# GeGLU feed-forward on one core: two pairs of f tiles share one run of plain products in the gate and up stage

## The chip, the cores and the metric

One Trainium2 chip, one core of it. The metric is the device time of one launch in microseconds. Inside a core, TensorE (PE in the profile) multiplies, with its weight loads shown as PEld; VectorE (DVE), ScalarE (ACT) and GpSimd (POOL) work elementwise; SyncE (SP) and ACT issue the transfers. The eight banks of PSUM, 128 x 512 fp32 each, hold what PE accumulates.

## The reference

```python
def _gelu(x):
    return jax.nn.gelu(x, approximate=True)
B, S, D, F = 1, 2048, 1024, 3584          # bfloat16 throughout
def reference(x, w_gate, w_up, w_down):
    return (_gelu(x @ w_gate) * (x @ w_up)) @ w_down
```

## The kernel before

**The halves.** The 2048 tokens are done in two halves (`h` = 0, 1) of 1024. Each half has a gate and up stage, which leaves `hT` = gelu(gate) x up with f on the partitions, and then a down stage (`down_group`, L703, two groups of 512 tokens) that multiplies by `w_down`. A half is two blocks of 512 tokens, kept transposed in `xT`.

**Seven products in place of eight.** Both stages cut their matrices in 2 x 2 blocks and form the result from seven block products. In the gate and up stage one such 2 x 2 problem is a *pair* of f tiles (2 x 128 columns of the weights) by the two token blocks, with D cut in two halves of four 128-row pieces. It is done once for gate (j = 0) and once for up (j = 1). The products are:

- M1 and M2, **plain**: bf16 weight blocks by bf16 `xT`;
- M5, M6, M7, M3 and M4, **of sums**: a sum of weight blocks (`s1`, `s2`, `s3`, `s4`, or a plain copy `a22`) by a sum of x blocks (`t1`, `t2`, `t3`, `b22`, `t4`), both kept as fp32r (fp32 in the profile's rows).

One product for one j is four matmuls of 128 x 128 by 128 x 512 (`mm`, L413) that accumulate in one bank. So a pair takes 2 x 2 plain products (16 matmuls) and 2 x 5 products of sums (40 matmuls). There are 14 pairs in each half; the first pair of half 0 is done apart, without sums, in `first_pair_units`.

**What happens to the products of a pair.** ACT copies M1 from its bank to bank set Q (L468); M2 accumulates on M1 where it stands, and gelu on ACT (L283) and the multiplication on DVE (L288, `mult`) take that result out. M6 accumulates on the copy in Q, and ACT copies the sum to set R (L464). M5 goes to set V and ACT copies it to a tile in SBUF (L458, `m5`). DVE adds `m5` to Q (L436), M3 accumulates there; M7 accumulates on R, DVE adds `m5` to that into V (L436); M4 accumulates on R. Each of the three results leaves through a gelu and a `mult`.

**Bank sets.** P, V, Q and R are two banks each (one for each j). Even pairs start their M1 in banks 0 and 1, odd pairs in 2 and 3, so that M2 of one pair can be held back.

**Order of PE.** The order on every engine is the order of the program (`on` chains the instructions of an engine). `pair_quads` does M1 of a pair, then M2 of the pair *before* (`pending`), and then the ten products of sums. So a run of 16 plain matmuls and a run of 40 matmuls of sums take turns once for each pair: 12 times after pair 1 of half 0, and 14 times in half 1. Most pairs take M6 ahead of M5.

**Preparing the next pair.** While PE does the products of sums of one pair, `prep` makes the sums of the next: POOL does `s1`, `s2`, `s3`, `s4` for both j, eight instructions (L385), and ACT the two copies `a22` (L398). There is one place in `s_mem` for each sum, so each can be made only when PE has read the old one.

**What rides along in half 0.** DVE also forms differences of `w_down` blocks for later (`stage_step`, L630, 42 of them, three for each of 14 units) that SP stores to `t_dram` (L632). Their inputs come by `stage_load` (L616) into three tiles of `wd_sb`. SP loads the x of the next half (`stage_x`, `store_x`). The next 512 columns of both weights come in two 1 MB transfers that ACT issues (`load_w`, L160), two pairs (one *chunk*) ahead.

**The end of a half.** In pair 13 SP loads the rows of `w_down` for the down stage (`load_b22` L554, `load_wd_rows` L550). Rows 8 to 13 and the first blocks of `b22` go over the memory of the last weight chunk, and blocks 4 to 13 of `b22` over that of the gelu results.

Of the kernel before, what the change touches and what calls it, by code (L numbers as in the profile page):

```python
# [34 lines left out]
def kernel(  # L35
# [8 lines left out]
    nc = tc.nc  # L44
# [355 lines left out]
    S_NAMES = ("s1", "s2", "s3", "s4", "a22")  # L400


    pending = []

    def pair_quads(hT, h, pair, nxt, then):

        key = (h, "p", pair)
        f0 = 2 * pair

        def mm(bank, j, lhs, rhs, start):  # L410
            for c in range(KH):
                pe(
                    nc.tensor.matmul(  # L413
                        banks[bank][:],
                        lhsT=lhs[:, c, :],
                        rhs=rhs[:, c, :],
                        start=start and c == 0,
                        stop=c == KH - 1,
                        skip_group_check=True,
                    )  # L420
                )

        def done(name):
            for f in then.get(name, ()):
                f()

        def prep(j, name):
            if nxt is not None:
                s_sum(nxt[0], nxt[1], j, name)

        def s(j, name):
            return ssum[(h, pair, j, name)]

        def add_m5(dst, src):
            dve(
                nc.vector.tensor_tensor(  # L436
                    out=banks[dst][:], in0=banks[src][:], in1=m5[j][:], op=ALU.add
                )
            )

        b11 = xT[0][:, half(0), :]
        b21 = xT[0][:, half(1), :]
        m5 = [None, None]
        g = {}
        P_, V_ = (PB, VB) if pair % 2 == 0 else (VB, PB)

        def m2():
            for j in range(2):
                mm(P_[j], j, block(key, j, 0, 1), b21, False)
                if j == 0:  # L450
                    g[0] = gelu(banks[P_[0]], nxt is None)
                else:
                    mult(hT, g[0], banks[P_[1]], f0, 0)

        def do_m5(j):
            mm(V_[j], j, s(j, "s1"), tsum["t1"], True)
            m5[j] = m_pool.tile([P, TB], F32, name=f"m5_{j}")
            act(nc.scalar.copy(out=m5[j][:], in_=banks[V_[j]][:]))  # L458
            if not eager:
                prep(j, "s1")  # L460

        def do_m6(j):
            mm(QB[j], j, s(j, "s2"), tsum["t2"], False)
            act(nc.scalar.copy(out=banks[RB[j]][:], in_=banks[QB[j]][:]))  # L464

        for j in range(2):
            mm(P_[j], j, block(key, j, 0, 0), b11, True)
            act(nc.scalar.copy(out=banks[QB[j]][:], in_=banks[P_[j]][:]))  # L468
        behind = len(pending) > 0
        eager = not behind and "m2" in then  # L470
        if behind:

            pending.pop()()
        done("m2 of last")
        if behind:
            if nxt is None:
                m2()
                done("m2")
            else:
                pending.append(m2)  # L480
            order = (do_m6, 0), (do_m6, 1), (do_m5, 0), (do_m5, 1)
        elif eager:
            m2()
            done("m2")
            order = (do_m5, 0), (do_m5, 1), (do_m6, 0), (do_m6, 1)
        else:
            pending.append(m2)
            order = (do_m5, 0), (do_m6, 0), (do_m6, 1), (do_m5, 1)
        for f, j in order:
            f(j)  # L490
            if (f, j) == (do_m6, 1):
                done("m6")
        for j in range(2):
            add_m5(QB[j], QB[j])
            if not eager:
                prep(j, "s2")
        done("m5")
        if eager:
            pool_behind_dve()
            for name in ("s1", "s2"):  # L500
                for j in range(2):
                    prep(j, name)
        for j in range(2):
            mm(RB[j], j, s(j, "s3"), tsum["t3"], False)
            add_m5(V_[j], RB[j])
            prep(j, "s3")
            if j == 0:
                g[1] = gelu(banks[V_[0]], nxt is None)
            else:
                mult(hT, g[1], banks[V_[1]], f0 + 1, 1)  # L510
        done("m7")
        for j in range(2):
            mm(QB[j], j, s(j, "s4"), tsum["b22"], False)
            prep(j, "s4")
            if j == 0:
                g[2] = gelu(banks[QB[0]], nxt is None)
            else:
                mult(hT, g[2], banks[QB[1]], f0, 1)
        done("m3")
        for j in range(2):  # L520
            mm(RB[j], j, s(j, "a22"), tsum["t4"], False)
            prep(j, "a22")
            if j == 0:
                g[3] = gelu(banks[RB[0]], nxt is None)
            else:
                mult(hT, g[3], banks[RB[1]], f0 + 1, 0)

        done("m4")

    SEQ = ("t1", "t2", "t3", "b22", "t4")
# [345 lines left out]

    for h in range(NH):
        hT = hT_pool.tile([P, KF, SH], BF16, name="hT")
        first_pair = 0
        if h == 0:
            first_pair_units(hT)
            first_pair = 1
            xs = [(tb, kd) for tb in (1, 0) for kd in range(KD)]
            new_x(1)
            stage_load(0)  # L890
            stage_load(1)
        for pair in range(first_pair, NPAIR):
            then = {}
            if pair % PPG == 0 and (pair // PPG + 1) * PPG < NPAIR:
                key = (h, pair // PPG + 1)

                if key not in chunks:
                    new_chunk(key)
                    for j, at in enumerate(("m2 of last", "m3")):
                        then[at] = [lambda j=j: load_w(key, j, 0, KD, act)]  # L900
            if h == 0 and pair < PPG:
                then = {
                    "m2": [lambda j=j: s_sum(0, pair, j, "a22") for j in range(2)]
                    + [lambda: t_sum("t4", 0, KH // 2)],
                    "m5": [lambda: t_sum("t4", KH // 2, KH)],
                }
            if h == 0 and pair >= PPG:

                n = [min(4 * (pair - PPG + d), NSTEP) for d in range(3)]
                steps = [lambda k=k: stage_step(k) for k in range(n[0], n[1])]  # L910
                new = range((n[1] + 2) // 3, (n[2] + 2) // 3)

                then["m2 of last"] = (
                    then.get("m2 of last", [])
                    + steps[:2]
                    + [lambda q=q: stage_x(hT, *q) for q in xs[:2]]
                )
                then["m7"] = [store_x] + [lambda i=i: stage_load(i) for i in new]
                then["m4"] = steps[2:]
                xs = xs[2:]  # L920
            if pair == NPAIR - 2:

                then.setdefault("m2 of last", []).extend(
                    [lambda: load_wd_rows(0, 4), lambda: load_wd_rows(4, 8)]
                )
            if 6 < pair < 11:
                i = 2 * pair - 8
                then.setdefault("m6", []).append(
                    lambda i=i: s_down(hT, 0, "s3", i, i + 2)
                )  # L930
            if pair == NPAIR - 1:
                then |= {
                    "m2 of last": [
                        lambda: load_b22(4, NS),
                        lambda: early.append(
                            wd_pool.tile([P, WDT, D], BF16, name="wd_sb")
                        ),
                        lambda: s_down(hT, 0, "s3", 0, 4),
                    ],
                    "m6": [  # L940
                        lambda: s_down(hT, 0, "s1", 4, 8),
                        lambda: t_down(0, "t1", 4, 6),
                    ],
                    "m2": [
                        lambda: load_wd_rows(8, 10),
                        lambda: load_wd_rows(10, 12),
                        lambda: load_wd_rows(12, NS),
                        lambda: load_b22(0, 4),
                    ],
                    "m7": [lambda: s_down(hT, 0, "s1", 0, 4)],  # L950
                    "m3": [lambda: t_down(0, "t1", 0, 2)],
                    "m4": [
                        lambda: t_down(0, "t2", 0, NT2),
                        lambda: t_down(0, "t1", 2, 4),
                        lambda: t_down(0, "t1", 6, 8),
                        lambda: s_down(hT, 0, "s1", 8, NS),
                        lambda: t_down(0, "t1", 8, NS),
                    ],
                }
            pair_quads(  # L960
                hT, h, pair, (h, pair + 1) if pair + 1 < NPAIR else None, then
            )

        then0 = {"m5": [lambda: s_down(hT, 0, "s3", 4, 6)]}
        then1 = {}
# [75 lines left out]
```

## Time and profile before

| | us |
|---|---|
| median of 3 runs (lowest, highest) | 539.48 (539.43, 539.6) |
| span of the profiled execution | 538.0 |
| what the runs' median has beyond that span | 1.48 |
| PE busy / PEld busy | 532.4 / 377.9 |
| DVE / ACT / POOL busy | 364.2 / 263.5 / 244.4 |
| gate and up of half 0, from pair 3 on | 43.4 to 183.2 |
| down of half 0 | 183.2 to 271.2 |
| gate and up of half 1 | 271.2 to 447.0 |
| down of half 1 | 447.0 to 538 |

The page gives a span for the profiled execution and no time of its own beyond it, so the span is set beside the runs. PE's clock is granted in full in all slices. PE's rows are the starts and modelled ends of matmuls; they overlap (a matmul of 0.39 us follows the one before by 0.23 us), so the busy share says little, and the distance between starts says how fast PE goes. A few matmul records are missing: of each run of 16 plain matmuls the trace has 15.

### The profile page before, as it was taken

The numbers are of one execution on the slowest core, as the hardware profiler recorded it, in microseconds if no ns is written. First come the engines' busy times: TensorE is split into PE (matmuls) and PEld (weight loads), VectorE is DVE, ScalarE is ACT, GpSimd is POOL, SyncE is SP. The second block draws the span as 40 slices with busy tenths as digits, with TensorE's granted clock in tenths as the row PEclk, the third lists the DMA queues.
The fourth block names the chain that finished last, engine by engine and source line by source line (L and its number), as shares of the span: only waits on it lengthen the run. The fifth ranks groups of instructions, "written<-read, shape, count | busy, mean of one in ns | idle before, by whom it ended". The sixth has DMA issues, their size and how long they took to land.

```text
span 538.0 us, 7084 instructions
## 1 busy us (share of the span) xinstructions
PE 532.4 (99%) x2352; PEld 377.9 (70%) x2388; DVE 364.2 (68%) x476; ACT 263.5 (49%) x447; POOL 244.4 (45%) x212
## 2 busy tenths in 40 slices
PE   9999999999999999999999999999999999999997
PEld 4577776666776686777776677777777766866866
DVE  1988777788775997989574334444444469969861
ACT  2555555555555329117465555555555552462280
POOL 0699877777776000000056776666777730000000
PEclk9999999999999999999999999999999999999999
DMA  9946876785815977789950405041322448677846
GB/s 205 323 128 195 207 252 185 238 262 197 291 61 200 361 239 246 237 279 308 324 171 1 156 1 158 15 142 57 100 78 80 155 133 284 220 246 252 293 141 212
DMA packets 92547, 102.70 MB, mean 191 GB/s; under 512 B 18656, under 2 KB 67424, under 8 KB 92512
## 3 DMA queue, kind: packets, MB, share of 16 engines
q1 hardware_dynamic: 69568, 80.23, 46.0%
q10 hardware_dynamic: 22944, 22.02, 13.4%
q8 instruction: 19, 0.31, 0.2%
q14 instruction: 16, 0.13, 0.1%
HBM read 85.98 MB, written 12.58 MB: 183 GB/s over the span
## 4 chain that ended last, share of the span: by engine, by line
PE 99%; issue 0%; ACT 0%; ACTq 0%
PE bank L413 63%; PE bank L703 33%; PE bank L264 3%; PE bank L202 1%; PE bank L308 0%; ACT bank L468 0%; ACT o_sb L759 0%; ACTq L468 0%
## 5 line engine op out<-in xcount | busy, mean ns | idle before, releaser
L413 PE MATMUL bank<-t_mem,s_mem 128*128 128x512 f32 x1056 | 249.6, 394 | 0.0
L413 PEld LDWEIGHTS bank<-t_mem,s_mem 128*128 128x128 f32 x1056 | 198.1, 188 | 44.1 <-DVE bank L436 0.4
L385 POOL TENSOR_TENSOR s_mem<-w_mem 128x512 fp32r<-128x512 bf16 x102 | 120.3, 1201 | 190.7 <-DVE t_mem L259 102.8
L703 PE MATMUL bank<-t_mem,s_mem 128*128 128x512 f32 (+1 forms) x548 | 127.2, 391 | 0.0
L288 DVE TENSOR_TENSOR hT<-w_mem,bank 128x512 bf16<-128x512 f32 x104 | 71.3, 687 | 79.9 <-PE bank L413 45.7
L703 PEld LDWEIGHTS bank<-t_mem,s_mem 128*128 128x128 f32 x548 | 102.4, 188 | 22.1 <-issue 0.2
L436 DVE TENSOR_TENSOR bank<-bank,m 128x512 f32<-128x512 f32 x108 | 69.9, 694 | 45.2 <-ACT m L458 43.7
L413 PE MATMUL bank<-xT,w_mem 128*128 128x512 bf16 x405 | 96.5, 380 | 1.4
L283 ACT ACTIVATE w_mem<-bank 128x512 f32<-128x512 f32 x104 | 61.8, 596 | 52.9 <-DVE bank L436 35.8
L413 PEld LDWEIGHTS <-w_mem 128*128 128x128 bf16 x432 | 40.2, 98 | 51.6 <-issue 6.8
L385 POOL TENSOR_TENSOR s_mem<-w_mem,s_mem 128x512 fp32r<-128x512 bf16 x52 | 65.8, 1285 | 0.0
L605 DVE TENSOR_TENSOR t_mem<-w_mem 128x1024 fp32r<-128x1024 bf16 x56 | 65.6, 1219 | 0.0
L385 POOL TENSOR_TENSOR s_mem<-s_mem,w_mem 128x512 fp32r<-128x512 f32 x52 | 60.9, 1192 | 0.0
L464 ACT COPY bank<-bank 128x512 f32<-128x512 f32 x54 | 30.8, 570 | 38.9 <-PE bank L413 38.9
L398 ACT CAST s_mem<-w_mem 128x512 fp32r<-128x512 bf16 x54 | 33.1, 615 | 30.6 <-PE bank L413 29.1
L675 DVE TENSOR_TENSOR s_mem<-hT 128x512 fp32r<-128x512 bf16 x52 | 34.2, 686 | 10.2 <-PE bank L703 9.4
L458 ACT COPY m<-bank 128x512 f32<-128x512 f32 x54 | 31.8, 589 | 17.5 <-PE bank L413 17.5
L703 PEld LDWEIGHTS <-hT 128*128 128x128 bf16 x224 | 21.3, 98 | 26.6 <-issue 2.1
L468 ACT COPY bank<-bank 128x512 f32<-128x512 f32 x54 | 30.7, 570 | 12.7 <-PE bank L413 12.7
L630 DVE TENSOR_TENSOR o_sb<-wd_sb,o_sb 128x512 fp32r<-128x512 bf16 x28 | 31.5, 1126 | 0.5
L768 ACT CAST o_sb<-bank 128x512 bf16<-128x512 f32 x27 | 14.8, 585 | 33.9 <-PE bank L703 33.9
L602 ACT CAST t_mem<-w_mem 128x1024 fp32r<-128x1024 bf16 x28 | 26.9, 1048 | 0.0
(45 smaller groups left out, 238.6 us busy)
## 6 DMA issues: line engine op xcount, KB each, us to landing
t_mem<-t_dram SPq DMA_DIRECT2D x56, 512.0 KB, 5.2
w_mem<-in_w_gate_dram ACTq DMA_DIRECT2D x10, 1024.0 KB, 5.5
w_mem<-in_w_up_dram ACTq DMA_DIRECT2D x10, 1024.0 KB, 5.5
wd_sb<-in_w_down_dram SPq DMA_DIRECT2D x28, 256.0 KB, 4.5
t_dram<-o_sb SPq DMA_DIRECT2D x28, 256.0 KB, 2.4
wd_sb<-in_w_down_dram SPq DMA_DIRECT2D x12, 512.0 KB, 7.7
w_mem<-in_w_down_dram SPq DMA_DIRECT2D x4, 1024.0 KB, 6.6
w_mem<-in_w_down_dram SPq DMA_DIRECT2D x8, 512.0 KB, 8.3
```

Of the source, the lines that this page charges most:

```text
L283: act(nc.scalar.activation(out=g_sb, in_=ps[:], func=ACT.Gelu_apprx_tanh))
L288: nc.vector.tensor_tensor(out=hT[:, fc, tb * TB : (tb + 1) * TB], in0=g_sb, in1=ps[:], op=ALU.mult,)
L385: pool(nc.gpsimd.tensor_tensor(out=t, in0=in0, in1=in1, op=op))
L398: act(nc.scalar.copy(out=t, in_=a(1, 1)))
L413: nc.tensor.matmul(banks[bank][:], lhsT=lhs[:, c, :], rhs=rhs[:, c, :], start=start and c == 0, stop=c == KH - 1, skip_group_check=True,)
L436: nc.vector.tensor_tensor(out=banks[dst][:], in0=banks[src][:], in1=m5[j][:], op=ALU.add)
L458: act(nc.scalar.copy(out=m5[j][:], in_=banks[V_[j]][:]))
L464: act(nc.scalar.copy(out=banks[RB[j]][:], in_=banks[QB[j]][:]))
L605: dve(nc.vector.tensor_tensor(out=t, in0=in0, in1=in1, op=ALU.subtract))
L630: dve(nc.vector.tensor_tensor(out=t, in0=in0, in1=in1, op=ALU.subtract))
L675: dve(nc.vector.tensor_tensor(out=t, in0=in0, in1=in1, op=op))
L703: nc.tensor.matmul(banks[bank][:, c0:c1], lhsT=lhs(i, u), rhs=rhs(i)[:, c0:c1], start=start and i == 0, stop=stop and i == NS - 1, skip_gr ...
```

## The change

`pair_quads` becomes `quads`, which takes both pairs of a chunk (`members`). It does M1 of both pairs and then M2 of both in one run of 32 plain matmuls, and after it the ten products of sums of the first pair and the ten of the second. `pending` is gone. Half 0 has pair 1 alone, as before, and then six such groups; half 1 has seven. The bank sets follow: in a group the first pair starts in P and copies its M1 to Q, the second starts in R and copies to V; then both use P for M5 and R for the copy of M6. All pairs take M6 ahead of M5, but for pair 1 of half 0 and the first group of half 1, which take M5 first.

What rides along is moved with it. Of the eight `stage_step` of a group four now stand on DVE behind M1 of both pairs and ahead of the two `mult` of the plain run, and two at the start of the sums of each pair (before, two stood behind M2 and two behind M4 in each pair). `stage_load` runs as tiles come free, and three are issued at the start, not two. The chunk loads, the loads of `x` and the `w_down` loads of the last two pairs stand at the start of a pair's sums ("start"), where they stood behind M2 of the pair before ("m2 of last").

```diff
-    def pair_quads(hT, h, pair, nxt, then):
+    def quads(hT, h, members, nxt, thens, m5_first):
...
+        for n, pair in enumerate(members):
+            after = (h, members[n + 1]) if n + 1 < len(members) else nxt
+            first_ = (PB, RB)[n] if len(members) > 1 else VB
+            run.append((pair, after, thens[n], first_, (QB, VB)[n]))
...
-        P_, V_ = (PB, VB) if pair % 2 == 0 else (VB, PB)
-
-        def m2():
+        for pair, _, _, first_, q_ in run:
             for j in range(2):
-                mm(P_[j], j, block(key, j, 0, 1), b21, False)
+                mm(first_[j], block((h, "p", pair), j, 0, 0), b11, True)
+                act(nc.scalar.copy(out=banks[q_[j]][:], in_=banks[first_[j]][:]))
+        done(0, "m1")
+        for pair, _, _, first_, _ in run:
+            for j in range(2):
+                mm(first_[j], block((h, "p", pair), j, 0, 1), b21, False)
                 if j == 0:
-                    g[0] = gelu(banks[P_[0]], nxt is None)
+                    g = gelu(banks[first_[0]])
                 else:
-                    mult(hT, g[0], banks[P_[1]], f0, 0)
+                    mult(hT, g, banks[first_[1]], 2 * pair, 0)
+
+        V_, R_ = PB, RB
+        for n, (pair, after, then, _, Q_) in enumerate(run):
...
+            done(n, "start")
+            if m5_first:
+                order = (do_m5, 0), (do_m5, 1), (do_m6, 0), (do_m6, 1)
             else:
-                pending.append(m2)
-            order = (do_m6, 0), (do_m6, 1), (do_m5, 0), (do_m5, 1)
...
-            stage_load(0)
-            stage_load(1)
-        for pair in range(first_pair, NPAIR):
+            for i in range(3):
+                stage_load(i)
...
+        def run_loads():
+            while loads and 3 * (loads[0] - 2) <= NSTEP - len(steps):
+                stage_load(loads.pop(0))
...
+        for lead in range(begin, NPAIR, PPG):
+            members = range(lead, lead + PPG)
...
+            if lead + PPG < NPAIR and key not in chunks:
+                new_chunk(key)
+                for j, at in enumerate(("start", "m3")):
+                    add(0, at, lambda j=j, key=key: load_w(key, j, 0, KD, act))
+            if h == 0:
+                add(0, "m1", lambda: run_steps(4))
+                for n in range(PPG):
+                    add(n, "start", lambda: run_steps(2), run_loads, run_x)
+                    add(n, "m7", store_x, run_loads)
...
+            quads(hT, h, members, nxt, thens, lead == 0)
```

## The prediction

> **What bounds the kernel now.** I read the page first: part 1 for the busy shares, part 4 for the chain that ended last.
>
> ```profile
> span 538.0 us, 7084 instructions
> ...
> PE 532.4 (99%) x2352; PEld 377.9 (70%) x2388; DVE 364.2 (68%) x476; ACT 263.5 (49%) x447; POOL 244.4 (45%) x212
> ...
> PE 99%; issue 0%; ACT 0%; ACTq 0%
> PE bank L413 63%; PE bank L703 33%; PE bank L264 3%; PE bank L202 1%; PE bank L308 0%; ACT bank L468 0%; ACT o_sb L759 0%; ACTq L468 0%
> ```
>
> The chain is PE from end to end, and the list of waits has one for PE, 0.8 us at the start. No wait is there to be removed, so the change can gain only what PE itself loses between matmuls. The timeline of PE shows that: start, length, and number of each run in half 0.
>
> ```profile
> 68.48 3.63 PE L413 MATMUL bank<-xT,w_mem 128*128 128x512 bf16 x15
> 71.75 9.44 PE L413 MATMUL bank<-t_mem,s_mem 128*128 128x512 f32 x40
> 81.04 3.63 PE L413 MATMUL bank<-xT,w_mem 128*128 128x512 bf16 x15
> 84.31 9.44 PE L413 MATMUL bank<-t_mem,s_mem 128*128 128x512 f32 x40
> 93.60 3.63 PE L413 MATMUL bank<-xT,w_mem 128*128 128x512 bf16 x15
> ```
>
> A pair takes 81.04 - 68.48 = 12.56 us, and the next one 12.56 again. How much of it is matmul, I take from two windows inside the runs, away from their ends (PE's timeline from 74.2 to 80.9, and from 81.7 to 84.0):
>
> ```profile
> 74.01 7.19 PE L413 MATMUL bank<-t_mem,s_mem 128*128 128x512 f32 x31
> ```
>
> ```profile
> 81.48 2.75 PE L413 MATMUL bank<-xT,w_mem 128*128 128x512 bf16 x12
> ```
>
> The last matmul of each row is 0.39 or 0.38 us long, so the distance between starts is (7.19 - 0.39) / 30 = 0.2267 us for sums and (2.75 - 0.38) / 11 = 0.2155 us for plain. (Over a longer run: pair 13 has eight more plain matmuls and lasts 14.29 us, so 1.73 / 8 = 0.216.) 40 x 0.2267 + 16 x 0.216 = 9.07 + 3.46 = 12.52. **Each pair loses 12.56 - 12.52 = 0.04 us** in going from plain to sums and back: a few matmuls next to each turn start 5 to 10 ns late. With 0.2155 the loss would be 0.045, with rounding the other way 0.035.
>
> **What the change removes.** The same 432 plain matmuls and 1080 of sums are left, and no operation is added on any engine. Turns: before, 1 (pair 1) + 12 + 14 = 27 rounds of a plain run and a run of sums; after, 1 + 6 + 7 = 14. 13 rounds less x 0.04 = **0.5 us** (0.035 to 0.045: 0.46 to 0.59). The ends for the price of a round are 0, if the loss goes with the products and not with the turn, and 0.045. I take 0.04, since it is the same in the two pairs shown and in half 1 (the plain runs start at 12.56 us there too), where DVE and POOL are far less busy.
>
> The Trainium skill, "TensorE: Matmul & The Clock Gate", section "Back-to-back issue gap", gives N / 2.4 + 2.5 ns between matmuls, 215.8 ns for 512 columns, and knows no price for a change of operand type. The plain row agrees (216); the 227 of sums and the 40 ns it does not have, and by the rule alone the change would be worth nothing: 539.5.
>
> **What is moved, and whether it stays hidden.** I write a group's clock from its first plain matmul. The plain run ends at 6.9; the sums of the first pair run to 16.0 and those of the second to 25.1, each product for one j 0.91 us. The period of two pairs was 25.12, so the work per period is unchanged on each engine and only its place can hurt.
>
> *Banks.* A plain product lasts 0.86, an ACT copy 0.57: the four copies are done by 4.1, and M2 of the first pair starts at 3.46 on a bank copied by 1.5. The second pair starts M1 in R at 1.73; the last gelu and `mult` on R end by 0.75. At the turn from first to second pair M6 goes into V, copied long before, and its copy goes to R at 16.9, against a `mult` on R that ends at 16.8. No bank makes PE wait as long as DVE is in time.
>
> *DVE in half 0.* This is the tight place, because four `stage_step` now stand ahead of two `mult`. Their price depends on POOL:
>
> ```profile
> 43.80 0.69 DVE L288 TENSOR_TENSOR hT<-w_mem,bank 128x512 bf16<-128x512 f32 x1 [1.30 <-ACT w_mem L283]
> 44.40 1.73 DVE L630 TENSOR_TENSOR o_sb<-wd_sb,o_sb 128x512 fp32r<-128x512 bf16 x1
> 46.05 1.64 DVE L630 TENSOR_TENSOR o_sb<-wd_sb 128x512 fp32r<-128x512 bf16 x1
> 47.62 0.67 DVE L288 TENSOR_TENSOR hT<-w_mem,bank 128x512 bf16<-128x512 f32 x1
> 48.22 2.65 DVE L630 TENSOR_TENSOR o_sb<-wd_sb,o_sb 128x512 fp32r<-128x512 bf16 x2
> ```
>
> One step takes 0.68 (the least of L630) with POOL idle and up to 1.73 (the most) with POOL at work. At 1.55 each, four steps run from 0.75 to 7.0; the two `mult` to 8.4. They are due when M5 of up starts in P, at 9.6, and when the copy of M6 of up must be in R for M7, at 11.4 less 0.57. The two steps at "start" then meet an idle POOL (below): 8.4 + 1.4 = 9.8, and the first add of `m5`, whose input is there at 10.2, is in time. It is due at 12.4 (M3). In the second pair two contended steps end at 16.8 + 3.1 = 19.9, the `m5` adds follow to 21.3, due at 21.5 and 22.4. The cover is 0.9 us or more.
>
> The skill's "SBUF — State Buffer", section "SBUF: two separate sides", says that DVE with two SBUF inputs and GpSimd lock each other out for whole instructions. The rows agree (0.68 against 1.73, about one POOL instruction of 1.15 more). By it four steps could cost 4 x 1.83 = 7.3 us as an estimate, ending the two `mult` at 9.4, still in time.
>
> *POOL.* Sums for the second pair could be made over 12.56 us; now they are due 3.46 us sooner. They start when M5 of gate has been read, as in the first row of POOL below (87.49, 3.18 after the sums began at 84.31).
>
> ```profile
> 50.27 2.73 POOL L385 TENSOR_TENSOR s_mem<-w_mem 128x512 fp32r<-128x512 bf16 x2
> ...
> 87.49 2.29 POOL L385 TENSOR_TENSOR s_mem<-w_mem 128x512 fp32r<-128x512 bf16 x2 [3.06 <-PE bank L413]
> 89.74 2.32 POOL L385 TENSOR_TENSOR s_mem<-s_mem,w_mem 128x512 fp32r<-128x512 f32 x2
> 92.01 2.29 POOL L385 TENSOR_TENSOR s_mem<-w_mem 128x512 fp32r<-128x512 bf16 x2
> 94.26 2.73 POOL L385 TENSOR_TENSOR s_mem<-w_mem,s_mem 128x512 fp32r<-128x512 bf16 x2
> ```
>
> The eight take 96.99 - 87.49 = 9.5 us; the slowest eight I find (44.43 to 55.28) 10.9. From 6.9 + 3.2 = 10.1 they end at 19.6 to 21.0. `s2` of gate, the third, is due at 16.0 and done by 13.5 to 14.2; the last, `s4` of up, is due at 16.0 + 6.35 = 22.3. Cover 1.3 us at the slowest. The sums for the next group then have 6.9 us more than before.
>
> *Loads on the way.* ACT issues the chunk loads at 7 and 14, and they land 5.5 us later (part 6); POOL reads them from 19.3 on. SP issues `stage_load` behind the steps at "start", at some 10.5, and they land 4.5 us later; the first step that needs one of the same group comes at 17.5. Covered.
>
> *`w_down` rows at the end of a half.* SP's timeline in half 1, pair 13's sums beginning at 437.73:
>
> ```profile
> 437.17 0.37 SPq L554 DMA_DIRECT2D w_mem<-in_w_down_dram  x1
> 437.71 1.91 SPq L550 DMA_DIRECT2D w_mem<-in_w_down_dram  x3
> 439.71 0.53 SPq L554 DMA_DIRECT2D w_mem<-in_w_down_dram  x1
> ```
>
> After, the first of these waits for the last `mult` of pair 12, 0.8 us into pair 13's sums, and the others for POOL's last sums, 2.1 and 3.3 us into them. With the 8.3 us of part 6 the rows are there by 11.6; the down stage's M1 begins at 9.1 and comes to row 8 sixteen matmuls later, at 12.5. Cover 0.9 us.
>
> **Sum.** All moves cost nothing, 0.5 us goes: span 538.0 to 537.5, and with the 1.48 us that the runs' median has beyond the span **539.0 us**, 0.1% less.
>
> **The rivals.**
>
> *A, no gain*: the late starts belong to something else than the turn, or a one-time wait of up to 1 us (the first group, where DVE comes late from pair 1) eats the gain: 539.2 to 540.0. For it: the price was never seen apart from one arrangement. Against: it repeats to 0.01 us.
>
> *B, slower by DVE*: all six steps ahead of the first `m5` add are contended and take 1.73. Then 0.75 + 4 x 1.73 + 1.38 + 2 x 1.73 = 12.5, the adds end at 13.2 and 13.9, due at 12.4 and 13.3: PE waits 0.8 us in each of the five groups with eight steps, + 4.0 - 0.5 = 543.0. It decides from a mean of 1.6 us for a step. For it: rows of 1.73 and 1.64 in a sequence. Against: POOL has nothing to do from 6.9 to 10.1, and the mean of L630 is 1.13.
>
> *C, slower by POOL*: eight sums at 1.6 us each, 12.8 from 10.1, are 0.6 us late for M3; five groups, + 3.0 - 0.5 = 542.0. It decides from 1.53 each; the mean is 1.2.
>
> *D, `w_down` late*: 2 us in each half, + 4 - 0.5 = 543.0, if the loads take 9.2 us.
>
> **Chances.** Forecast 0.70; A 0.13; B 0.07; C 0.04; D 0.03; a gain over 1.1 us from a term that I hold at nothing 0.03. About 0.2% (1.08 us) is what a measurement of this kernel can tell from no change: within it are the forecast and A, 0.83; faster 0.03; slower B, C and D, 0.14. The range goes from 538.6 (0.59 gained, and gone as well what pair 1 loses, whose run of 40 takes 9.78 us against 9.44) to 540.2, the end of A and some.
>
> **What would show it.** Right: PE's timeline in steps of 25.08 us, plain runs of 31 or 32 records, 14 turns, no wait for PE. A: steps of 25.12. B: waits of PE's matmuls of sums on the add of DVE, in half 0 only. C: waits on POOL. D: a gap between the down stage's matmuls near 187 and 450. If PE waits nowhere and the time is not within 0.3 us of 539.0, the price of a turn is wrong.

## The result and the profile after

The changed kernel takes **545.6 us** (544.43 to 546.42, four runs) against 539.54: 1.0107 times as long, 95% interval 1.0095 to 1.0119. Its profiled execution took 545.85 us with a span of 544.0. So it lost 6.1 us (6.0 by the spans of the two profiled executions) where 0.5 was to be gained; the prediction's range was 538.6 to 540.2.

The page of the changed kernel, parts 1 and 4:

```profile
PE 535.7 (98%) x2388; PEld 378.6 (70%) x2388; DVE 374.1 (69%) x476; ACT 263.0 (48%) x447; POOL 250.2 (46%) x212
...
PE 65%; DVE 1%; issue 0%; ACT 0%; DVEq 0%
PE bank L415 32%; PE bank L691 32%; DVE s_mem L663 0%; DVE wd_sb L663 0%; DVE t_mem L593 0%; DVE bank L431 0%; ACT o_sb L747 0%; DVEq L663 0%
```

The chain is no longer PE alone: three lines of DVE are in it (L663 the differences for the down stage, L593 the `t1` differences of the down stage, L431 the adds of `m5`), and with them part 4 names the engine. The chain as the page has it reaches back only to 183 us; so it holds the last two of the five waits below, and its shares add up to 66%. The list of waits says who waits for it (who waits, for whom, us in total, times, longest):

```profile
PE bank L415 <- DVE bank L431: 4.6, 5, 1.5
```

Where the five waits are, the timeline of PE tells:

```profile
82.67 7.08 PE L415 MATMUL bank<-xT,w_mem 128*128 128x512 bf16 x32
89.40 14.88 PE L415 MATMUL bank<-t_mem,s_mem 128*128 128x512 f32 x64
105.00 3.89 PE L415 MATMUL bank<-t_mem,s_mem 128*128 128x512 f32 x16 [0.71 <-DVE bank L431]
108.73 7.08 PE L415 MATMUL bank<-xT,w_mem 128*128 128x512 bf16 x32
115.46 14.88 PE L415 MATMUL bank<-t_mem,s_mem 128*128 128x512 f32 x64
131.04 3.91 PE L415 MATMUL bank<-t_mem,s_mem 128*128 128x512 f32 x16 [0.70 <-DVE bank L431]
...
156.69 3.89 PE L415 MATMUL bank<-t_mem,s_mem 128*128 128x512 f32 x16 [0.28 <-DVE bank L431]
...
183.50 3.91 PE L415 MATMUL bank<-t_mem,s_mem 128*128 128x512 f32 x16 [1.47 <-DVE bank L431]
...
357.67 18.51 PE L415 MATMUL bank<-t_mem,s_mem 128*128 128x512 f32 x80
376.02 7.08 PE L415 MATMUL bank<-xT,w_mem 128*128 128x512 bf16 x32
382.75 18.51 PE L415 MATMUL bank<-t_mem,s_mem 128*128 128x512 f32 x80
...
449.27 3.91 PE L415 MATMUL bank<-t_mem,s_mem 128*128 128x512 f32 x16 [1.48 <-DVE bank L431]
```

A clean group is 80 matmuls of sums in one piece, and the distance from 357.67 to 382.75 is 25.08 us: what was forecast for a group. In the five others the 80 break behind the 64th, that is ahead of M3 of the *second* pair: in the pairs 7, 9 and 11 and, in both halves, 13. Taken as the distances between the starts of matmuls less the usual 0.227, the five cost 0.96, 0.94, 0.52, 1.71 and 1.72 us (the matmul behind the wait starts late as well and is counted), some 5.8 us together.

By stages, from the starts of their first matmuls in the two timelines:

| from | before | after | difference |
|---|---|---|---|
| start to the first run after pair 1 | 32.52 | 32.51 | 0.0 |
| gate and up, half 0, from there | 150.72 | 154.74 | +4.0 |
| down, half 0 | 87.93 | 88.11 | +0.2 |
| gate and up, half 1 | 175.84 | 177.66 | +1.8 |
| down, half 1, to the end | 91.0 | 91.0 | 0.0 |

### The profile page after: what moved, and what is told of

The parts are those of the page before. It is cut to its first block, busy times and chain, and to the rows that moved or that the text cites. A ratio compares the mean times of both kernels' runs of the same rounds, so it can differ in the third digit from the quotient of the medians.

```text
span 544.0 us, 7036 instructions
## 1 busy us (share of the span) xinstructions
PE 535.7 (98%) x2388; PEld 378.6 (70%) x2388; DVE 374.1 (69%) x476; ACT 263.0 (48%) x447; POOL 250.2 (46%) x212
## 4 chain that ended last, share of the span: by engine, by line
PE 65%; DVE 1%; issue 0%; ACT 0%; DVEq 0%
PE bank L415 32%; PE bank L691 32%; DVE s_mem L663 0%; DVE wd_sb L663 0%; DVE t_mem L593 0%; DVE bank L431 0%; ACT o_sb L747 0%; DVEq L663 0%
## 5 line engine op out<-in xcount | busy, mean ns | idle before, releaser
L415 PE MATMUL bank<-t_mem,s_mem 128*128 128x512 f32 x1056 | 246.1, 392 | 4.6 <-DVE bank L431 4.6
L385 POOL TENSOR_TENSOR s_mem<-w_mem 128x512 fp32r<-128x512 bf16 x102 | 123.8, 1234 | 191.4 <-DVE t_mem L259 99.0
L431 DVE TENSOR_TENSOR bank<-bank,m 128x512 f32<-128x512 f32 x108 | 69.6, 692 | 40.8 <-ACT m L469 34.4
L385 POOL TENSOR_TENSOR s_mem<-w_mem,s_mem 128x512 fp32r<-128x512 bf16 x52 | 67.9, 1326 | 3.4 <-PE bank L415 3.4
L593 DVE TENSOR_TENSOR t_mem<-w_mem 128x1024 fp32r<-128x1024 bf16 x56 | 65.5, 1216 | 0.0
L663 DVE TENSOR_TENSOR s_mem<-hT 128x512 fp32r<-128x512 bf16 x52 | 37.2, 747 | 8.3 <-PE bank L691 8.3
L618 DVE TENSOR_TENSOR o_sb<-wd_sb,o_sb 128x512 fp32r<-128x512 bf16 x28 | 33.2, 1185 | 0.6
```

Source lines behind the costliest of these rows:

```text
L385: pool(nc.gpsimd.tensor_tensor(out=t, in0=in0, in1=in1, op=op))
L415: nc.tensor.matmul(banks[bank][:], lhsT=lhs[:, c, :], rhs=rhs[:, c, :], start=start and c == 0, stop=c == KH - 1, skip_group_check=True,)
L431: nc.vector.tensor_tensor(out=banks[dst][:], in0=banks[src][:], in1=m5[:], op=ALU.add)
L593: dve(nc.vector.tensor_tensor(out=t, in0=in0, in1=in1, op=ALU.subtract))
L618: dve(nc.vector.tensor_tensor(out=t, in0=in0, in1=in1, op=ALU.subtract))
L663: dve(nc.vector.tensor_tensor(out=t, in0=in0, in1=in1, op=op))
```

## The experiments

**The theories.** *Q*: DVE has more instructions ahead of the first `m5` add of a group's second pair than fit before M3. *P*: the same instructions would fit, but POOL makes its sums at that time, and the two slow each other. *S*, the rival outside DVE: POOL's sums come too late. The trace speaks against S at once, as PE waits for DVE in all five places, but a wait for several semaphores names only the last. Here are the three instructions that stand ahead of the adds in pair 7, before and after. Before:

```profile
98.06 0.68 DVE L630 TENSOR_TENSOR o_sb<-wd_sb,o_sb 128x512 fp32r<-128x512 bf16 x1
98.67 0.68 DVE L630 TENSOR_TENSOR o_sb<-wd_sb 128x512 fp32r<-128x512 bf16 x1
99.27 0.68 DVE L675 TENSOR_TENSOR s_mem<-hT 128x512 fp32r<-128x512 bf16 x1
```

After:

```profile
99.73 2.94 DVE L618 TENSOR_TENSOR o_sb<-wd_sb,o_sb 128x512 fp32r<-128x512 bf16 x2
102.59 1.65 DVE L663 TENSOR_TENSOR s_mem<-hT 128x512 fp32r<-128x512 bf16 x1
104.17 2.48 DVE L431 TENSOR_TENSOR bank<-bank,m 128x512 f32<-128x512 f32 x4
```

Before, POOL was idle from 96.99 to 100.05; after, it works without a gap from 92.58 to 112.4. This is DVE around the last of the five waits, and POOL at the same time:

```profile
443.24 2.94 DVE L663 TENSOR_TENSOR wd_sb<-hT 128x512 fp32r<-128x512 bf16 x2
446.10 1.28 DVE L663 TENSOR_TENSOR s_mem<-hT 128x512 fp32r<-128x512 bf16 x2
447.30 1.21 DVE L593 TENSOR_TENSOR t_mem<-w_mem 128x1024 fp32r<-128x1024 bf16 x1
448.44 1.88 DVE L431 TENSOR_TENSOR bank<-bank,m 128x512 f32<-128x512 f32 x3
```

```profile
440.60 2.29 POOL L385 TENSOR_TENSOR s_mem<-w_mem 128x512 fp32r<-128x512 bf16 x2
442.87 2.76 POOL L385 TENSOR_TENSOR s_mem<-w_mem,s_mem 128x512 fp32r<-128x512 bf16 x2
```

From 443.2 DVE is never idle until the adds. The two `s3` differences take 2.94 us beside POOL's `s4`; before, where POOL had finished at 435.67, they took 1.28:

```profile
437.06 1.28 DVE L675 TENSOR_TENSOR wd_sb<-hT 128x512 fp32r<-128x512 bf16 x2
```

After, the sums began at 432.91 + 9.07 = 442.0, and M3 was due 5.44 later (the 24 matmuls of M6, M5 and M7), at 447.4; the first add ends at 449.1. POOL's `s4` was ready at 445.6, 1.8 us before M3 was due, so it was not `s4` that M3 waited for. All runs below name the ratio to the kernel before, measured beside them.

### One part of the placement undone: the difference behind M6

```diff
-                if 6 < pair < 11:
-                    i = 2 * pair - 8
+                if pair in (6, 8, 10, 12):
+                    i = pair
                     add(n, "m6", lambda i=i: s_down(hT, 0, "s3", i, i + 2))
```

> One part of the placement undone: the VectorE difference s3 for the down stage, that stood behind M6 in pairs 7, 8, 9 and 10, is put behind M6 in pairs 6, 8, 10 and 12, so always in the first pair of a group. Theory Q (VectorE has more to do ahead of the first m5 add of the second pair than fits before M3): the waits of PE before M3 near 104 and 130 us (0.96 and 0.94 us beyond the normal distance, the next matmul included) go, those near 156 (0.5), 183 and 449 (1.7 each) stay; span about 544.0 - 1.9 = 542.1, ratio to the kernel before 1.007. Rival S (the sums of POOL come too late for M3): nothing changes, 544.0, since POOL's work is the same.

543.5 us, ratio 1.0067 (1.0053 to 1.008), span 541.7. The waits in pairs 7 and 9 are gone, those of pair 13 are whole (1.72 and 1.71). The one in pair 11 went too, which was not expected, and one of 0.5 us came in pair 5, which has no such difference. So the two steps of "start" alone are at the edge, and it depends on how they fall beside POOL's instructions. (The wait in pair 11 is absent from the next two runs as well, which do not touch that pair; so its going in a run proves nothing.) S is out: POOL's work was the same.

### Pair 13 alone

```diff
                         lambda: load_wd_rows(4, 8),
...
+                        lambda: s_down(hT, 0, "s3", 0, 4),
                     )
...
                     lambda: load_b22(4, NS),
...
-                    lambda: s_down(hT, 0, "s3", 0, 4),
...
                     lambda: s_down(hT, 0, "s1", 4, 8),
-                    lambda: t_down(0, "t1", 4, 6),
                 )
+                add(n, "m5", lambda: t_down(0, "t1", 4, 6))
```

The first of these places is the start of pair 12's sums, the second that of pair 13's.

> Pair 13 alone: the two s3 differences leave the start of its sums for the start of pair 12's, and one t1 difference of the down stage goes from ahead of the m5 adds to behind them. Theory Q: 1.3 to 2.9 us and 1.2 us leave VectorE's queue ahead of the adds, which were 1.7 us late; the two waits near 183 and 449 us go, the three others stay; span about 544.0 - 3.4 = 540.6, ratio 1.004. Rival S: no change. Rival P (it is only the contention of VectorE and POOL): the two s3 differences then cost 1.3 us instead of 2.9, and the waits go as well; this run does not tell P from Q.

541.87 us, ratio 1.0041 (1.0026 to 1.0056). Both waits in pair 13 are gone; pairs 7 and 9 keep theirs (0.3 and 1.1). The profiled execution was the fastest of its four, span 539.2; the median is what the forecast of 1.004 says.

### The same instructions without POOL beside them: `s4` of pair 13 left out

```diff
         def tt(in0, in1, op):
+            if pair == NPAIR - 1 and name == "s4":
+                return
```

> The changed kernel with one thing left out: POOL does not form the sums s4 of pair 13 in either half, so that M3 of that pair works on old values; the order of VectorE is untouched. Theory P (contention makes VectorE late): the two s3 differences at the start of pair 13's sums take 1.3 us in place of 2.9, and of the waits near 183 and 449 us about 1.6 of 1.7 us goes in each half; span about 544.0 - 3.3 = 540.7. Theory Q in its strict form (the number of instructions alone): both waits stay whole, 544.0. In between, each has its share. Rival S (POOL's s4 is what M3 waits for): both waits go whole too, but VectorE's adds would then still end after M3 began, which the trace would show.

541.82 us, ratio 1.0036 (1.0022 to 1.005), span 540.5. DVE's order is untouched, and pair 13 waits no more. Its queue in half 0:

```profile
177.41 1.28 DVE L665 TENSOR_TENSOR wd_sb<-hT 128x512 fp32r<-128x512 bf16 x2
178.61 1.29 DVE L665 TENSOR_TENSOR s_mem<-hT 128x512 fp32r<-128x512 bf16 x2
179.82 1.22 DVE L595 TENSOR_TENSOR t_mem<-w_mem 128x1024 fp32r<-128x1024 bf16 x1
180.95 2.48 DVE L433 TENSOR_TENSOR bank<-bank,m 128x512 f32<-128x512 f32 x4
```

The two differences take 1.28 again. The sums began at 176.2, M3 was due at 181.6, and the first add ends at 181.6. For pair 13 P holds and strict Q falls; but the queue is just as long as what fits.

### Nothing left out, only POOL moved

```diff
             done(n, "start")
+            if n == 1:
+                pool_behind_dve()
+                for j in range(2):
+                    s_sum(h, pair, j, "s4")
...
-                prep(j, "s4")
+                if n == len(run) - 1:
+                    prep(j, "s4")
```

> VectorE's order as in the changed kernel; only POOL is moved: the sums s4 of the second pair of a group are formed behind VectorE's work at the start of that pair's sums (POOL waits for the last of it) and not ahead of it. Nothing is left out. Theory P (the two slow each other, and that makes the m5 adds late): the steps and the s3 differences at that place take 0.68 us each again, the waits before M3 of the second pair shrink from 0.96, 0.94, 0.5, 1.7 and 1.7 us to a tenth or two, and in pair 13 to 0.1 at most; span 537.5 to 538.2. Theory Q in its strict form (instructions, not contention): all five waits stay, 544.0. Rival S: POOL, 2 us later with s4, makes PE wait for it before M3.

In pair 13 the loads of `w_down` rows stood ahead of the moved sums in the program, so `s4` was formed there from the overwritten chunk and after it had landed: PE waits 11.6 and 12.0 us and goes slower for a while behind each wait (last section). That makes 567.37 us (ratio 1.0513, 1.0498 to 1.0527) and belongs to the experiment, not to the change. The twelve pairs ahead of it tell what was asked. PE's timeline in half 0:

```profile
89.75 18.51 PE L415 MATMUL bank<-t_mem,s_mem 128*128 128x512 f32 x80
...
114.83 18.51 PE L415 MATMUL bank<-t_mem,s_mem 128*128 128x512 f32 x80
```

DVE in pair 7:

```profile
100.08 1.41 DVE L623 TENSOR_TENSOR o_sb<-wd_sb,o_sb 128x512 fp32r<-128x512 bf16 x2
101.41 0.68 DVE L668 TENSOR_TENSOR s_mem<-hT 128x512 fp32r<-128x512 bf16 x1
102.57 0.70 DVE L431 TENSOR_TENSOR bank<-bank,m 128x512 f32<-128x512 f32 x1 [0.48 <-ACT m L469]
```

With not one instruction of DVE moved, the three instructions take 0.7 us each again, the first add ends 1.0 us ahead of M3 (due at 104.3), the waits in pairs 7, 9 and 11 are gone, and every group of half 0 ahead of pair 13 takes 25.08 us. For pairs 7 and 9 this shows P; the wait in pair 11 went in other runs too. POOL, 2 us later with `s4`, makes PE wait nowhere in these pairs. Mended, with the loads behind the sums:

> As the run before in which POOL forms s4 of a group's second pair behind VectorE's work at the start of that pair's sums, but in pair 13 the loads of the rows of w_down that go over the weight chunk stand behind those sums and no longer ahead of them (there s4 was formed from the overwritten chunk, after a wait of 11.6 and 12.0 us for the loads). Theory P: the waits of 0.96, 0.94, 0.5, 1.7 and 1.7 us before M3 all but go, with VectorE's own order untouched: span 537.5 to 538.2, ratio 0.999 to 1.000. Theory Q in its strict form: 544. Rival S: PE waits on POOL before M3.

546.22 us, ratio 1.0113 (1.0099 to 1.0127). The first three waits are gone again, but pair 13 waits 2.5 us in each half, more than before: the expectation was wrong there. DVE in pair 13 of half 0:

```profile
175.05 1.29 DVE L669 TENSOR_TENSOR wd_sb<-hT 128x512 fp32r<-128x512 bf16 x2
177.71 2.24 DVE L669 TENSOR_TENSOR s_mem<-hT 128x512 fp32r<-128x512 bf16 x2 [1.38 <-POOL s_mem L385]
179.88 1.21 DVE L599 TENSOR_TENSOR t_mem<-w_mem 128x1024 fp32r<-128x1024 bf16 x1
```

The `s1` differences of the down stage go over the place of `s2`, which POOL reads for `s4`. So in pair 13 DVE hangs on POOL in a second way, and POOL made later makes DVE later. (The profiled execution, span 542.9 at a granted clock of 1.00, is the fastest of four; the other three are 1.5 to 1.6 us longer and have a mean granted clock of 0.996 or 0.997. Where their clock fell is in no profile.)

### The kernel before, with the same two differences moved

```diff
                     "m2 of last": [
...
-                        lambda: s_down(hT, 0, "s3", 0, 4),
                     ],
...
                     "m2": [
...
+                        lambda: s_down(hT, 0, "s3", 0, 4),
```

> The kernel before with one thing moved: the two s3 differences of pair 13 from behind M2 of pair 12 to behind M2 of pair 13, that is from inside the plain run to the start of the sums, where the changed kernel has them; POOL has done its sums by then. If the plain run ahead of each pair's sums was VectorE's cover: the queue ahead of the m5 adds grows by 1.3 us, the adds start near 443.1 in place of 441.8 in half 1 and end 0.5 us behind M3's due time of 443.2, so PE waits some 0.5 us in each half: span 539.0, ratio 1.002. If place does not matter without POOL's contention: 538.0, ratio 1.000.

540.03 us, ratio 1.0 (0.9991 to 1.0009). No wait in pair 13: the adds start 4.6 us behind the sums' begin (443.37 against 438.76) and the first ends 0.1 us ahead of M3. My half microsecond was worked out from a row of the kernel before in which DVE still had idle gaps; they closed. So the place alone does not make PE wait; place and POOL together do. (The profiled execution, span 539.1, was the slowest of eleven; its late starts lie in pair 1 and in the down stage.)

### A run of plain products split in two, for the price of a turn

```diff
+        m2_last = pending.pop() if behind else None
...
             if (f, j) == (do_m6, 1):
+                if behind and nxt is not None:
+                    m2_last()
+                    done("m2 of last")
                 done("m6")
```

> The price of a turn, measured on the kernel before: M2 of the pair before, which stood behind M1 of a pair, goes between M6 and M5, so that the run of 16 plain matmuls becomes two of 8 in 22 of the pairs (3 to 12 of half 0, 1 to 12 of half 1). 22 turns more, the same matmuls. If a turn costs 0.04 us: span + 0.9, ratio 1.0016, and the period of a pair 12.60 in place of 12.56 us. If the late starts belong to the products and not to the turn: 12.56, ratio 1.000. VectorE's multiplication of M2 comes 1.8 us later in the pair, and 1.2 us of steps with it; a wait of PE before M3 would show it.

557.59 us, ratio 1.0332 (1.0318 to 1.0346). As a measure of the turn it failed: a pair takes 13.03 us in half 1 (306.70 to 319.73), but the added 0.47 us are spread over the pair (0.12 ahead of M6, 0.13 in it, the rest in the products behind the second plain run), and products now follow copies and gelus that had cover, so the price of a turn cannot be told from them. What it shows is the mechanism again: with DVE's multiplication and steps 1.8 us later, M3 comes 1.6 us late in exactly the pairs 7, 8, 9 and 10, the four with the difference behind M6:

```profile
100.75 4.03 PE L413 MATMUL bank<-t_mem,s_mem 128*128 128x512 f32 x16
106.23 2.08 PE L413 MATMUL bank<-t_mem,s_mem 128*128 128x512 f32 x8 [1.45 <-DVE bank L436]
```

### Towards a version without the waits

Both moves of the first two runs, and three steps at the start of the first pair's sums with one at the second's:

```diff
-                    add(n, "start", lambda: run_steps(2), run_loads, run_x)
+                    add(n, "start", lambda n=n: run_steps((3, 1)[n]), run_loads, run_x)
```

> Both moves, and of the steps that feed the scratch in memory three instead of two stand at the start of the first pair's sums (where POOL idles) and one instead of two at that of the second pair. Theory Q: no wait of PE is left in the gate and up stage, and what remains is the gain from 13 turns fewer at 0.04 us: span 537.5, time 539.0, ratio 0.999 (539.48 before). If a turn is worth nothing: ratio 1.000, span 538.0. Rival S: 544.0 still.

540.38 us, ratio 1.0013 (1.0001 to 1.0025). The waits in second pairs are gone; three smaller ones (0.57, 0.43 and 0.32 us) stand ahead of M3 of the *first* pairs 6, 8 and 10, which now have three steps and the difference. I had put too much there. So the steps were spread:

```diff
-                add(0, "m1", lambda: run_steps(4))
+                add(0, "m1", lambda: run_steps(3))
...
-                    add(n, "start", lambda: run_steps(2), run_loads, run_x)
+                    add(n, "start", lambda n=n: run_steps((2, 0)[n]), run_loads, run_x)
+                    add(n, "m3", lambda: run_steps(1))
...
+                if pair in (5, 7, 9, 11):
+                    i = pair + 1
+                    add(n, "start", lambda i=i: s_down(hT, 0, "s3", i, i + 2))
```

> The changed kernel with VectorE's extra work spread by where it has room: of the steps three (not four) behind M1, two at the start of the first pair's sums, none at the start of the second's, and one behind M3 of each pair (seven for a group, 42 in six groups); the s3 differences at the start of the second pair's sums in pairs 5, 7, 9 and 11; pair 13 as in the run of that alone. Theory Q and P both: no wait of PE before M3 is left, and 13 turns fewer remain: span 537.5 against 538.0, ratio 0.999. If turns are worth nothing: 1.000. If ahead of M3 contention still makes VectorE late somewhere: some tenths of a us for each of the waits listed.

540.29 us, ratio 1.0012 (1.0003 to 1.0021). Half 0 is clean up to pair 13, with groups of 25.08 us; 0.6 us of late starts remain in pair 13, where `s1` waits for POOL's `s4`, and 0.3 in the first group of half 1. The last version takes these two out (the edit is against the spread version):

```diff
-                    lambda: s_down(hT, 0, "s1", 4, 8),
+                    lambda: t_down(0, "t1", 4, 6),
                 )
-                add(n, "m5", lambda: t_down(0, "t1", 4, 6))
-                add(n, "m7", lambda: s_down(hT, 0, "s1", 0, 4))
+                add(n, "m7", lambda: s_down(hT, 0, "s1", 0, 8))
...
-            quads(hT, h, members, nxt, thens, lead == 0)
+            quads(hT, h, members, nxt, thens, False)
```

> The spread order with two things more: in pair 13 only one t1 difference is left between M6 and the m5 adds, and the four s1 differences stand behind M7 (the first of them waited for POOL to have read its place, 1.4 us, with the adds behind it); and the first group of half 1 takes M6 ahead of M5 as all others do (M5 first cost 0.34 us there: 25.42 against 25.08 for a group). Expected from the spread run's 538.4: less 0.67 and 0.34, span 537.4, ratio 0.998 to 0.999. If a turn were worth nothing the groups would take 25.12, and 537.9.

**539.27 us, ratio 0.999** (0.9981 to 0.9999), span 536.9 in the profiled execution, which was the fastest of eleven (the others 537.2 to 538.0). PE's only wait is that at the start of the kernel, as in the kernel before:

```profile
PE bank L202 <- PEq L1035: 0.8, 1, 0.8
```

It beats both kernels, by 0.5 us and 6 us, and by what the prediction gave for 13 turns; the interval only just excludes no gain. The trace is the firmer evidence: the gate and up stages (that of half 0 taken from behind pair 1) last 150.50 and 175.56 us, against 150.72 and 175.84 before, 0.50 us less together. (The other 0.6 us by which this span is shorter lie ahead of them, at the start of the kernel, and are no part of the gain.) Twelve of the thirteen groups take 25.08 us (157.36 to 182.44 is the one with pair 13), the first 25.10.

## Why the prediction was wrong

- **13 turns less at 0.04 us: right as a sum.** A group without a wait takes 25.08 us in the changed kernel, as forecast, where two pairs took 25.12, and the version without waits gains 0.5 us. That it is the turn itself, and nothing else in the new order, that had cost the 0.04 us was not shown apart: the run with more turns could not tell.
- **Banks, ACT and chunk loads: right.** PE waits for none of them. The `w_down` rows left no wait either.
- **POOL: right as to PE**, which waits for it nowhere, also when it makes `s4` later. Wrong in what it does to DVE, below.
- **DVE in half 0: the step that failed.** "In the second pair two contended steps end at 16.8 + 3.1 = 19.9 ... The cover is 0.9 us or more." The working left out an instruction, the `s3` difference behind M6 in pairs 7 to 10, which falls on the second pair of a group in 7 and 9. In pair 7 DVE does two steps (2.94 us) and this difference (1.65, beside POOL; 0.68 alone), and the adds begin at 104.17, 5.7 us behind the start of those sums and 0.3 us after M3 was due. With 1.65 us more, the prediction's own working would have had the first add some 0.75 us too late; the waits cost 0.96 and 0.94. The forecast also took 1.73 us for the worst step, and in pair 11, where there is no such difference, one took 2.49: that wait, 0.52 us, came in some runs and not in others.
- **Pair 13: no DVE queue was written out at all**, only SP's loads. Five instructions stand ahead of the adds there, two `s3`, two `s1` and a `t1`, 5.2 us from 443.24 on. Before, the two `s3` began in the plain run of 24 matmuls ahead of the sums, with POOL at rest. The grouping takes away that plain run from every second pair, and with it both DVE's time and POOL's: POOL finishes 3.6 us into the sums, where it had finished 2.1 us ahead of them. This is 3.4 of the 5.8 us.
- **Rival B named the mechanism**, DVE late for M3 because POOL contends, and its place, half 0. It priced it at 543.0 and gave it 0.07. It put the waits in the first pair, behind the burst of four steps, and "in half 0 only"; the burst was never late, the second pair was, and in half 1 too.
- The first group of half 1, with M5 ahead of M6, takes 25.42 us, 0.3 more than the others, which the prediction did not look for; with M6 first it takes 25.08.

The sum, by the lengths of the groups: the five with a wait take 26.06, 26.07, 25.62, 26.83 and 26.84 us, together 6.0 more than five clean ones (5.8 in the waits, 0.2 in late starts near them); + 0.3 for the first group of half 1, + 0.2 for late starts in the down stage of half 0, - 0.5 for the turns = 6.0 us, by which the spans differ.

## What to carry to other kernels

When an order is regrouped, write out the whole queue of every in-order engine for every kind of place, the last pair and the pairs with extras too, from the order of the changed program and not from the diff: a plain run that looks like PE's work was DVE's cover. Price each instruction beside what runs next to it *after* the change: 0.68 us became 1.65 because POOL's work moved over it. A loss by such a move is not against the idea; with some of DVE's instructions put elsewhere, and M6 first in one group more, the same grouping gained what it should.

## What the runs showed of the hardware

**A step that let two POOL instructions pass.** In pair 11 of the changed kernel, DVE and POOL:

```profile
151.86 2.49 DVE L618 TENSOR_TENSOR o_sb<-wd_sb,o_sb 128x512 fp32r<-128x512 bf16 x1
154.27 1.66 DVE L618 TENSOR_TENSOR o_sb<-wd_sb 128x512 fp32r<-128x512 bf16 x1
```

```profile
151.49 2.32 POOL L385 TENSOR_TENSOR s_mem<-w_mem,s_mem 128x512 fp32r<-128x512 bf16 x2
153.77 3.18 POOL L385 TENSOR_TENSOR s_mem<-w_mem 128x512 fp32r<-128x512 bf16 x2
```

The step, 0.68 us alone, starts 0.4 us into the first of POOL's two instructions and ends 0.5 us behind the second. So it seems to have waited for both: 2.49 less 0.68 is 1.81 us, about what was left of the two. POOL's next ones, 1.16 alone, then take 1.6 each. The Trainium skill ("SBUF — State Buffer", section "SBUF: two separate sides") says that, where DVE has two inputs in SBUF, one of the two engines holds the ports for its whole instruction while the other blocks. That fits; the estimate of 1.83 drawn from it, one POOL instruction and the step, does not: in this row the blocked one was not next.

**PE slows after a long wait.** In the run with the overwritten chunk PE stood still from 179.87 to 191.09 and, in half 1, for about as long up to 468.13. The windows around these waits show its clock (stretch, length, busy time and number of PE, PEld, DVE, ACT and POOL, granted clock, DMA share, GB/s):

```profile
179.90:183.90 4.00, 0.00 (x0) 0.00 (x0) 0.00 (x0) 0.00 (x0) 0.00 (x0) 1.00 1.04 389
183.90:191.09 7.19, 0.00 (x0) 0.03 (x1) 3.27 (x5) 0.00 (x0) 2.31 (x2) 0.50 0.36 124
191.09:194.10 3.01, 3.01 (x7) 2.43 (x8) 2.92 (x6) 1.19 (x2) 0.00 (x0) 0.50 0.00 0
194.10:196.24 2.14, 2.14 (x11) 1.53 (x10) 2.14 (x4) 0.60 (x1) 0.00 (x0) 1.00 0.25 31
468.13:474.00 5.87, 5.87 (x14) 4.61 (x15) 5.36 (x8) 1.57 (x3) 0.00 (x0) 0.50 0.15 29
```

In the first wait the granted clock fell to 0.50 after 4.0 us of standing still. It stayed there for 3.0 us behind the first wait and 5.9 us behind the second; the 16 matmuls behind them took 5.3 and 6.6 us in place of 3.9. In the profiled executions of the other runs, waits of up to 2.2 us left the clock at 1.00. Whether a wait of 2.2 us can lower it is open: three executions without a profile (POOL's sums moved, the loads behind them) had a mean clock of 0.996 or 0.997.
